# Routing attention and feed-forward block: the first sequence's first layer in written order, a second buffer under the accumulating transfers, and another order at the start

## The chip, the cores and the metric

The kernel runs on one core of one Trainium2 chip. The metric is the device time in microseconds (us); the time before is 976.38 us, the median of 3 runs (975.72 to 977.27). The traced execution spans 973.6 us; all trace times count from its start. TensorE is called PE (PEld for its weight loads), VectorE DVE, ScalarE ACT, GpSimd POOL, SyncE SP. "L387" is line 387 of the kernel before.

## The reference

Attention in which a query sees only the keys whose nearest centroid is the same as its own, then a layer norm and a two-layer feed-forward with a residual:

```python
# q, k, v: (4, 8, 768, 64); centroids: (8, 16, 64)
q_n = q / (norm(q) + 1e-6); k_n = k / (norm(k) + 1e-6); c_n = centroids / (norm(centroids) + 1e-6)
q_assign = argmax(einsum('bhsd,hcd->bhsc', q_n, c_n)); k_assign = argmax(einsum('bhsd,hcd->bhsc', k_n, c_n))
scores = where(q_assign == k_assign, q @ k.T / 8, -1e9)
attn   = softmax(scores) @ v            # -> x: (4, 768, 512)
xn = (x - mean) / sqrt(var + 1e-6) * g_ln
out = x + maximum(xn @ w_ch1, 0) @ w_ch2    # w_ch1: (512, 2048), w_ch2: (2048, 512), float64 in memory
```

## The kernel before

The kernel works through 16 pairs of heads (4 sequences, 4 pairs each) and then, for each sequence, through the feed-forward. Both layers of the feed-forward use a scheme with seven products of half-size blocks instead of eight. The text needs four parts of it.

**The start.** Before the first pair can be masked, the centroids must be normed and turned, similarities computed, the best cluster of every row marked in `onehot`, and that be turned into two mask tiles:

```python
load(0, "q")
nc.scalar.dma_start(out=c_sb, in_=centroids.rearrange("h c d -> (h c) d"))
load(0, "kv")                       # pair 0: halves of q and k alternate on the SP and ACT queues
# ... identity, masks, constants: memsets on GpSimd
def norm_centroids(part):
    if part == 0:   # DVE: squares, sum, lower bound          -> c_ss
    elif part == 1:
        nc.scalar.activation(c_nrm, c_ss, AF.Sqrt)
        nc.scalar.activation(warm, c_nrm, AF.Exp, scale=0.0)   # only brings Exp's table in
    else:           # DVE: five small operations              -> c_sb normed

with tc.manual_schedule(engines=order):      # order = PE, DVE, ACT: these run as written
    norm_centroids(0); prep_transpose(0, 0); load(1, "q")
    norm_centroids(1); prep_transpose(0, 1); load(1, "k")
    norm_centroids(2)
    scores(0, "qk", ("qk",))        # score step 0, its q k product alone
    turn_centroids()
    scores(1, "qk", ("qk",))
    prep_sims(0); prep_turn(0); prep_route(0)       # similarities, turned, one-hot
    prep_transpose(1, 0)            # pair 1's q
    # ... loads
    prep_onehot(0); prep_mask(0, 0); prep_mask(0, 1)    # m on DVE for pair 0; two masks on ACT
    scores(0, "qk", ("mask", "exp")); scores(1, "qk", ("mask", "exp"))
    # ... all 192 score steps, the weighted sums and the weight chunks between them
```

**Weights.** Each of the 32 chunks (128 x 512 float64) is turned into float32 on DVE: the high words give a rounded part that is written to `w`, the low words a rest in `tb`, which a transfer adds to `w`. `tb` is free again when that transfer has landed. 23 chunks are converted in the attention, the last 9 in sequence 0's first layer.

```python
def split_weight(m):                 # three DVE operations
    ta = pools["conv"].tile([P, WC], U32, tag="ta", name="ta")
    tb = pools["conv"].tile([P, WC], U32, tag="tb", name="tb")      # the pool has one buffer
    # L238, L241: ta from the high words;  L244: tb from the high words
def join_weight(m):                  # three more
    # L253: w from ta and tb;  L257: tb from w;  L258: tb from the low words and tb
    nc.gpsimd.dma_start(out=w, in_=fb, accum_op=ALU.add)            # fb is tb read as float32; L261
```

**First layer.** Seven parts for each j of 0 to 7; a product is four matmuls. One bank x takes parts 1, 6, 7 and 4 one after another, and ACT copies it out between them:

```python
def first_layer(b, j, part):
    if part == 1:   product(x, ..., True);  p1 = kept(x)        # kept: ACT copy, L724
    elif part == 2: product(y, ..., True);  add_relu(y + p1)    # DVE add, L729; appended to summed
    elif part == 6: product(x, s2, t2);     u2 = kept(x)
    elif part == 5: product(z, s1, t1, True)
    elif part == 7: product(x, s3, ...);    u3 = kept(x); add_relu(z + u3)
    elif part == 4: product(x, ...);        nc.scalar.activation(hidden, x, AF.Relu)    # L765
    elif part == 3: product(z, s4, ...);    add_relu(z + u2)
def relu(m):        # ACT: ReLU in place over the m oldest of summed, L737
def w1_sums(b, j):  # DVE: four sums of weight blocks s1..s4 for part 6, 5, 7, 3 of j, L572, two buffers
```

**The loop around it.** Only PE's order is fixed here; the scheduler orders DVE, ACT, SP and GpSimd:

```python
with tc.manual_schedule(engines={PE, DVE}):
    # j = 0: parts 1, 2, 6, 5, 7, the sums, the end of the last pair (finish(.., 0))
with tc.manual_schedule(engines={PE}):
    for b in range(B):
        for j in range(NFH):
            if j + 1 < NFH and (b or j): w1_sums(b, j + 1)
            for part, ahead in ((1, 0), (2, 0), (4, 1), (6, 0), (3, 1), (5, 0), (7, 0)):
                if j - ahead >= 0 and (b or j): first_layer(b, j - ahead, part)
            relu(max(0, len(summed) - 3))
            if b == 0 and j in (1, 3): finish(len(pairs) - 1, (j + 1) // 2)
            for m in within.pop(j, ()) if b == 0 else ():    # one chunk each for j = 1, 2, 3, 6, 7; two for 4 and 5
                split_weight(m); join_weight(m); load_weight(m + 2)
        # ... second layer (L802)
```

Of the kernel before, what the change touches and what calls it, by code (L numbers as in the profile page):

```python
# [19 lines left out]
def kernel(  # L20
# [11 lines left out]
    nc = tc.nc  # L32
# [86 lines left out]
    load(0, "q")  # L119

    c_sb = const.tile([H * NCL, D], F32, name="c_sb")
    nc.scalar.dma_start(out=c_sb, in_=centroids.rearrange("h c d -> (h c) d"))
    load(0, "kv")

    ident = const.tile([P, P], F32, name="ident")
# [32 lines left out]
    c_ss = const.tile([H * NCL, 1], F32, name="c_ss")  # L158
    c_nrm = const.tile([H * NCL, 1], F32, name="c_nrm")
    c_tmp = const.tile([H * NCL, 1], F32, name="c_tmp")  # L160
    warm = const.tile([P, 1], F32, name="warm")

    def norm_centroids(part):
        if part == 0:
            nc.vector.tensor_tensor(c_sq, c_sb, c_sb, ALU.mult)
            nc.vector.tensor_reduce(c_ss, c_sq, AX.X, ALU.add)

            nc.vector.tensor_scalar_max(c_ss, c_ss, 2.0 ** -100)
        elif part == 1:
            nc.scalar.activation(c_nrm, c_ss, AF.Sqrt)  # L170

            nc.scalar.activation(warm, c_nrm, AF.Exp, scale=0.0)
        else:

            nc.vector.reciprocal(c_tmp, c_nrm)
            nc.vector.scalar_tensor_tensor(
                out=c_tmp, in0=c_tmp, scalar=c_ss, in1=c_nrm, op0=ALU.mult, op1=ALU.add
            )
            nc.vector.tensor_scalar(c_nrm, c_tmp, 0.5, 1e-6, op0=ALU.mult, op1=ALU.add)
            nc.vector.reciprocal(c_tmp, c_nrm)  # L180
            nc.vector.tensor_scalar_mul(c_sb, c_sb, c_tmp)
# [50 lines left out]
    def split_weight(m):  # L232
        words = raws[m].bitcast(U32).rearrange("p (n w) -> p n w", w=2)
        hi = words[:, :, 1]
        ta = pools["conv"].tile([P, WC], U32, tag="ta", name="ta")
        tb = pools["conv"].tile([P, WC], U32, tag="tb", name="tb")

        nc.vector.tensor_scalar(  # L238
            ta, hi, 0x07FFFFFF, 3, op0=ALU.bitwise_and, op1=ALU.logical_shift_left
        )  # L240
        nc.vector.scalar_tensor_tensor(  # L241
            out=ta, in0=hi, scalar=0xC0000000, in1=ta, op0=ALU.bitwise_and, op1=ALU.bitwise_or
        )
        nc.vector.tensor_single_scalar(tb, hi, 0x7FF00000, op=ALU.bitwise_and)  # L244
        halves[m] = (ta, tb)
# [84 lines left out]
    def prep_onehot(n):  # L330
# [8 lines left out]
                )  # L339

        m = heads.tile([P, S], BF16, tag="m", name="m")
        if n:
            nc.scalar.activation(m, t[:, :S], AF.Identity, bias=far[:, 0:1], scale=far[:, 1:2])
        else:
            nc.vector.tensor_scalar(
                m, t[:, :S], far[:, 1:2], far[:, 0:1], op0=ALU.mult, op1=ALU.add
            )
        z = mask[n % 2]
        prepared[n]["oh"] = t
        prepared[n]["m"] = [(z[:D], m[:D]), (m[D:], z[D:])]  # L350
# [1 line left out]
    def prep_mask(n, j):  # L352
        t, z = prepared[n]["oh"], mask[n % 2]
        src, dst = ((D, 0), (Q, D + Q))[j]
        src, dst = slice(src, src + NCL), slice(dst, dst + NCL)
        nc.scalar.activation(  # L356
            z[dst], t[src, :S], AF.Identity, bias=far[src, 0:1], scale=far[src, 1:2]
        )

# [242 lines left out]
    with tc.manual_schedule(engines=order):  # L604
# [4 lines left out]
        prep_transpose(0, 1)  # L609
        load(1, "k")  # L610
        norm_centroids(2)
        scores(0, "qk", ("qk",))
        turn_centroids()
        scores(1, "qk", ("qk",))
        prep_sims(0)
        prep_turn(0)
        prep_route(0)
        prep_transpose(1, 0)
        load(2, "q")
        load_weight(0)  # L620
        load_weight(1)
        prep_onehot(0)
        prep_mask(0, 0)
        prep_mask(0, 1)
        scores(0, "qk", ("mask", "exp"))
        scores(1, "qk", ("mask", "exp"))
        for u in range(len(pairs) * slots):
            n, slot = divmod(u, slots)
            nxt = n + 1 < len(pairs)
# [222 lines left out]
            add_store(b, 0, tt, 1, st["u2", tt], st["z", tt])  # L852


    with tc.manual_schedule(engines={mybir.EngineType.PE, mybir.EngineType.DVE}):
        first_layer(0, 0, 1)
        first_layer(0, 0, 2)
        first_layer(0, 0, 6)
        finish(len(pairs) - 1, 0)
        w1_sums(0, 0, (2, 3))  # L860
        x_sum(0, 3)
        first_layer(0, 0, 5)
        first_layer(0, 0, 7)
        x_sum(0, 4)
        w1_sums(0, 1)

    with tc.manual_schedule(engines={mybir.EngineType.PE}):
        for b in range(B):
            st = {}
            if b:  # L870
                w1_sums(b, 0)
            for j in range(NFH):
                if j + 1 < NFH and (b or j):
                    w1_sums(b, j + 1)
                for part, ahead in ((1, 0), (2, 0), (4, 1), (6, 0), (3, 1), (5, 0), (7, 0)):
                    if j - ahead >= 0 and (b or j):
                        first_layer(b, j - ahead, part)
                relu(max(0, len(summed) - 3))
                if b == 0 and j in (1, 3):
                    finish(len(pairs) - 1, (j + 1) // 2)  # L880
                for m in within.pop(j, ()) if b == 0 else ():
                    split_weight(m)
                    join_weight(m)
                    load_weight(m + 2)
            if b == 0:
                rest.close()
                ffn = pool("ffn", 2)
            relu(len(summed))
# [240 lines left out]
```

## Time and profile before

| engine | busy, us | share of the span | instructions |
|---|---|---|---|
| PE | 945.2 | 97% | 4614 |
| PEld | 576.8 | 59% | 4614 |
| DVE | 611.1 | 63% | 1102 |
| ACT | 349.8 | 36% | 557 |
| POOL | 77.4 | 8% | 146 |

Busy time is the time in which an engine has an instruction under way; for PE, whose matmuls overlap, a busy stretch may still run at a lower granted clock. The mean granted clock is 0.988. In a line of the timeline stand the start and the length in us, engine, source line, operation, output and inputs, shapes, how many were merged, and in brackets the idle time of the engine before it with what ended it. A line of the waits holds who waited for whom, the time in all, how often, and the longest. The stages of the span: the start (0 to 24 us), the attention (to 366), sequence 0's first layer (to 456), its second layer and the three other sequences (to the end).

### The profile page before, as it was taken

How to read it: one execution, taken by the hardware profiler on the slowest of the kernel's cores; microseconds unless marked ns; L12 is line 12 of the kernel's file. 1: busy time of each engine (PE TensorE's matmuls, PEld its weight loads, DVE VectorE, ACT ScalarE, POOL GpSimd, SP SyncE). 2: the span in 40 equal slices, each digit the busy share in tenths (PEclk: the TensorE clock that was granted, in tenths of full speed). 3: DMA queues.
4: the chain of work that ended last, by engine and by line, in shares of the span. 5: the costliest groups of instructions: out<-in, count | busy, mean ns of one | idle time of the engine just before them, and what ended most of it. 6: DMA issues, size and time to landing. Idle time of an engine off the chain costs nothing.

```text
span 973.6 us, 12451 instructions
## 1 busy us (share of the span) xinstructions
PE 945.2 (97%) x4614; PEld 576.8 (59%) x4614; DVE 611.1 (63%) x1102; ACT 349.8 (36%) x557; POOL 77.4 (8%) x146
## 2 busy tenths in 40 slices
PE   5999999999999999888999999999999999999997
PEld 2444444444344445445888556888556888556886
DVE  3788889988798876665967344563344563344431
ACT  4666667667666662222100333000333000333000
POOL 1011212111112121111000000000000000000000
PEclk8999999999999999999999999999999999999999
DMA  7368789987887433542553000211000211000011
GB/s 174 82 150 208 179 191 206 209 181 161 158 168 150 111 77 93 130 98 54 168 173 103 1 0 2 96 66 65 1 1 5 92 66 66 1 0 6 29 39 39
DMA packets 178324, 92.48 MB, mean 95 GB/s; under 512 B 144352, under 2 KB 160848, under 8 KB 178256
## 3 DMA queue, kind: packets, MB, share of 16 engines
q1 hardware_dynamic: 168800, 76.20, 31.3%
q0 software_dynamic: 7712, 14.99, 7.6%
q8 instruction: 38, 0.62, 0.3%
q10 hardware_dynamic: 1744, 0.43, 0.2%
q14 instruction: 30, 0.25, 0.1%
HBM read 64.10 MB, written 19.10 MB: 85 GB/s over the span
## 4 chain that ended last, share of the span: by engine, by line
PE 88%; DMA 4%; issue 4%; DVE 1%; ACT 1%; POOL 0%; ACTq 0%; SPq 0%; POOLq 0%; DVEq 0%
PE s_ps L387 17%; PE x_ps L802 17%; PE a_ps L399 14%; PE x_ps L709 13%; PE z_ps L802 9%; PE z_ps L709 7%; PE y_ps L802 4%; PE y_ps L709 3%; DMA w<-tb 2%; PE den_ps L436 1%; PE sim_ps L293 1%; PE oh_ps L335 1%; PE simT_ps L309 1%; PE qk_ps L276 1%; DMA q_sb<-in_q_dram 1%
## 5 line engine op out<-in xcount | busy, mean ns | idle before, releaser
L382 ACT ACTIVATE e<-s_ps 128x768 f32<-128x768 f32 x192 | 151.6, 809 | 65.5 <-PE s_ps L387 64.4
L387 PE MATMUL s_ps<-t,t 64*128 64x384 f32 x768 | 158.1, 490 | 0.0
L399 PE MATMUL a_ps<-e,v_sb 128*64 128x384 f32 x768 | 144.8, 499 | 0.0
L416 DVE TENSOR_TENSOR es<-es,e 128x768 f32<-128x768 f32 x128 | 121.7, 951 | 21.1 <-ACT e L382 15.7
L737 ACT ACTIVATE h<-h 128x384 f32<-128x384 f32 x96 | 50.2, 523 | 166.8 <-DVE h L729 166.8
L399 PEld LDWEIGHTS a_ps<-e,v_sb 128*64 128x64 f32 x768 | 46.7, 136 | 88.2 <-issue 72.2
L802 PE MATMUL x_ps<-w2t,h 128*128 128x256 f32 x384 | 84.5, 379 | 0.0
L387 PEld LDWEIGHTS s_ps<-t,t 64*128 64x128 f32 x768 | 69.6, 192 | 20.7 <-issue 19.1
L802 PEld LDWEIGHTS x_ps<-w2t,h 128*128 128x128 f32 x384 | 72.7, 190 | 10.1
L387 PE MATMUL s_ps<-m,mask 64*128 64x384 bf16 x192 | 63.6, 331 | 2.8 <-ACT mask L356 1.9
L387 PE MATMUL s_ps<-mask,m 64*128 64x384 bf16 x192 | 63.4, 331 | 0.5 <-ACT mask L356 0.5
L572 DVE TENSOR_TENSOR ws<-w 128x256 f32<-128x256 f32 x64 | 24.5, 418 | 58.4 <-PE z_ps L709 58.4
L709 PE MATMUL x_ps<-xt,w 128*128 128x384 f32 x128 | 49.4, 510 | 7.9 <-ACT u L724 7.9
L729 DVE TENSOR_TENSOR h<-z_ps,u 128x384 f32<-128x384 f32 x64 | 35.2, 551 | 25.5 <-ACT u L724 15.8
L387 PEld LDWEIGHTS <-mask 64*128 64x128 bf16 x192 | 17.9, 94 | 55.9 <-issue 39.6
L709 PE MATMUL x_ps<-xt,ws 128*128 128x384 f32 x128 | 48.9, 506 | 2.1 <-ACT p L724 2.1
L813 DVE TENSOR_TENSOR o_sb<-x_ps,xb 128x256 f32<-128x256 f32 x48 | 20.0, 418 | 48.6 <-PE x_ps L802 48.6
L709 PE MATMUL z_ps<-xn,ws 128*128 128x384 f32 x128 | 47.1, 491 | 1.4 <-DVE h L729 1.4
L709 PE MATMUL x_ps<-xn,ws 128*128 128x384 f32 x128 | 46.7, 488 | 0.6 <-ACT u L724 0.5
L724 ACT COPY p<-x_ps 128x384 f32<-128x384 f32 x32 | 14.8, 464 | 90.1 <-PE x_ps L709 90.1
L709 PE MATMUL x_ps<-xn,w 128*128 128x384 f32 x128 | 46.6, 487 | 0.6 <-ACT late L425 0.6
L709 PE MATMUL z_ps<-xt,ws 128*128 128x384 f32 x128 | 46.6, 487 | 0.0
(137 smaller groups left out, 1378.7 us busy)
## 6 DMA issues: line engine op xcount, KB each, us to landing
raw<-in_moe_w_ch_dram SPq DMA_DIRECT2D x32, 512.0 KB, 4.9
w<-tb POOLq DMA_DIRECT2D x32, 256.0 KB, 5.2
v_sb<-in_v_dram SPq DMA_DIRECT2D x32, 192.0 KB, 3.9
xn<-xT_d SPq DMA_DIRECT2D x16, 384.0 KB, 5.2
xr<-x_d SPq DMA_DIRECT2D x24, 256.0 KB, 2.8
xb<-x_d SPq DMA_DIRECT2D x48, 128.0 KB, 2.2
out_dram<-o_sb SPq DMA_DIRECT2D x48, 128.0 KB, 1.7
k_sb<-in_k_dram SPq DMA_DIRECT2D x62, 96.0 KB, 4.6
```

The lines of the kernel that those rows point to most:

```text
L276: nc.tensor.transpose(t[:, c * P : (c + 1) * P], src[:, g * TH + c, :, :].rearrange("p h d -> p (h d)"), ident,)
L382: nc.scalar.activation(e, s[:, :, :HC], AF.Exp, scale=SCALE)
L387: nc.tensor.matmul(s[:, j, :HC], of_keys[:, keys], of_queries[:, cols], start=part == first, stop=part != first, skip_group_check=True,)
L399: nc.tensor.matmul(acc[j * D : (j + 1) * D, :HC], loaded[n]["v"][:, j, c, :], e[:, j, :], start=(c == 0), stop=(c == NT - 1),)
L416: nc.vector.tensor_tensor(es, es, soft.pop(i), ALU.add)
L572: nc.vector.tensor_tensor(t[:, i], x, y, op)
L709: nc.tensor.matmul(bank[:, :HC], lhs[:, c, :], rhs[:, c, :], start=first and c == 0, stop=c == NDH - 1, skip_group_check=True,)
L724: nc.scalar.copy(t, bank[:, :HC])
L729: nc.vector.tensor_tensor(h, bank[:, :HC], other, ALU.add)
L737: nc.scalar.activation(h, h, AF.Relu)
L802: nc.tensor.matmul(bank[:, :MH], hidden[lhs + (c,)][:, tt * P : (tt + 1) * P], rhs[:, c, :], start=first and c == 0, stop=c == NFH - 1, sk ...
L813: nc.vector.tensor_tensor(o, bank[:, :MH], x, ALU.add)
```

## The change

It is meant to keep PE from waiting in two places: at the start, where the first pair's masks are prepared, and in sequence 0's first layer, where weight chunks are converted beside the products. It does five things:

- the centroids are loaded over GpSimd's queue instead of ACT's;
- Sqrt's table is brought in by an activation on a constant, ahead of everything else on ACT, and the activation that brings Exp's table in no longer reads `c_nrm`;
- turning the centroids, the similarities and the turning of pair 0 come ahead of the first score products, pair 1's q transposes after the first two masked score steps, and pair 0's two masks go from ACT to DVE;
- `tb` gets two buffers;
- sequence 0's first layer is put, unit by unit, into the region whose order holds on PE, DVE and ACT: each chunk's conversion stands in two halves between named parts, and one ReLU after each of the parts 4, 6 and 3. For the other sequences the same function runs with only PE's order fixed.

The diff, cut to its core:

```diff
-    nc.scalar.dma_start(out=c_sb, in_=centroids.rearrange("h c d -> (h c) d"))
+    nc.gpsimd.dma_start(out=c_sb, in_=centroids.rearrange("h c d -> (h c) d"))
...
     warm = const.tile([P, 1], F32, name="warm")
+    nc.vector.memset(warm, 1.0)
+    nc.scalar.activation(warm, warm, AF.Sqrt)
...
             nc.scalar.activation(c_nrm, c_ss, AF.Sqrt)
-            nc.scalar.activation(warm, c_nrm, AF.Exp, scale=0.0)
+            nc.scalar.activation(warm, warm, AF.Exp, scale=0.0)
...
-        tb = pools["conv"].tile([P, WC], U32, tag="tb", name="tb")
+        tb = pools["conv"].tile([P, WC], U32, tag="tb", name="tb", bufs=2)
...
+    def shade(n, out, src, rows):      # used for m and for both masks
+        add, factor = far[rows, 0:1], far[rows, 1:2]
+        if n:
+            nc.scalar.activation(out, src, AF.Identity, bias=add, scale=factor)
+        else:
+            nc.vector.tensor_scalar(out, src, factor, add, op0=ALU.mult, op1=ALU.add)
...
         norm_centroids(2)
-        scores(0, "qk", ("qk",))
         turn_centroids()
-        scores(1, "qk", ("qk",))
         prep_sims(0)
         prep_turn(0)
+        scores(0, "qk", ("qk",))
         prep_route(0)
-        prep_transpose(1, 0)
-        load(2, "q")
...
         prep_mask(0, 1)
+        scores(1, "qk", ("qk",))
         scores(0, "qk", ("mask", "exp"))
         scores(1, "qk", ("mask", "exp"))
+        prep_transpose(1, 0)
+        load(2, "q")
...
+    def first_units(b, j):
+        chunks = within.pop(j, []) if b == 0 else []
+        for part, ahead in ((1, 0), (2, 0), (4, 1), (6, 0), (3, 1), (5, 0), (7, 0)):
+            if chunks and part in (1, 3):
+                split_weight(chunks[0])
+            if j >= ahead:
+                first_layer(b, j - ahead, part)
+            if part in (4, 6, 3):
+                relu(1)
+            if chunks and part in (2, 3):
+                m = chunks.pop(0)
+                join_weight(m)
+                load_weight(m + 2)
+            if part == 5 and j + 1 < NFH:
+                w1_sums(b, j + 1)
...
-    with tc.manual_schedule(engines={mybir.EngineType.PE, mybir.EngineType.DVE}):
+    with tc.manual_schedule(engines=order):
         # ... j = 0 as before
+        for j in range(1, NFH):
+            first_units(0, j)
+            if j in (1, 3):
+                finish(len(pairs) - 1, (j + 1) // 2)
```

More of the change, by code (lines that the diff above doesn't have):

```diff
@@ L341, in prep_onehot @@
         m = heads.tile([P, S], BF16, tag="m", name="m")
[L342 to L347, printed above, removed]
+        shade(n, m, t[:, :S], slice(0, P))
         z = mask[n % 2]
@@ L355, in prep_mask @@
         src, dst = slice(src, src + NCL), slice(dst, dst + NCL)
-        nc.scalar.activation(
-            z[dst], t[src, :S], AF.Identity, bias=far[src, 0:1], scale=far[src, 1:2]
-        )
+        shade(n, z[dst], t[src, :S], src)
+    def shade(n, out, src, rows):
[4 more added lines that the diff above has]
+            nc.vector.tensor_scalar(out, src, factor, add, op0=ALU.mult, op1=ALU.add)
     xT_d = [spill.tile([NDC, P, S], F32, name=f"xT_d{b}") for b in range(B)]
@@ L871 @@
                 w1_sums(b, 0)
[L872 to L885, printed above, removed]
+                for j in range(NFH):
+                    first_units(b, j)
+            else:
                 rest.close()
```

## The prediction

> **What bounds the kernel now.** I read the busy table first, then the stages, then the waits of the stages in which TensorE is not full, then the timeline there. The busy table gives PE 945.2 us of a span of 973.6 us, so at most 28 us can come from a better order; no matmul is added or taken away. The stages tell where those 28 us lie (columns: stretch, its length, then the busy time of PE, PEld, DVE, ACT, POOL, then the granted clock):
>
> ```profile
> 0.00:24.00 24.00, 13.96 (x58) 7.17 (x60) 7.17 (x20) 10.48 (x15) 4.85 (x34) 0.81 0.75 176
> 24.00:366.00 342.00, 341.61 (x2300) 142.29 (x2298) 293.59 (x431) 228.81 (x310) 62.13 (x98) 1.00 0.73 159
> 366.00:456.50 90.50, 79.29 (x232) 43.03 (x229) 57.47 (x128) 23.73 (x53) 9.59 (x13) 0.94 0.42 98
> 456.50:464.20 7.70, 6.34 (x25) 4.48 (x24) 5.96 (x14) 1.79 (x4) 0.84 (x1) 1.00 0.35 78
> 464.20:960.00 495.80, 495.80 (x1968) 373.01 (x1967) 245.61 (x510) 84.97 (x176) 0.00 (x0) 1.00 0.15 48
> ```
>
> PE idles 10.0 us in the first 24 us and 12.6 us around the first sequence's first layer (11.2 + 1.4); in the attention and from 464 us on it is full. Both holes also run partly at half clock (0.81 and 0.94). The change touches these two stages and no other.
>
> The size of the second hole follows from a comparison inside the trace. The first layer's units j = 1 to 7 take 81.58 us for sequence 0 (PE timeline, 374.96 to 456.54) and, with the same 196 matmuls, 63.21 us for sequence 1 (539.94 to 603.15), where nothing waits. From there to the 32 matmuls of the second layer the two take 7.66 us (456.54 to 464.20) and 6.03 us (603.15 to 609.18). Lost in sequence 0: 18.37 + 1.63 = 20.0 us. The granted clock explains 5.1 us of it (0.83, 0.93 and 0.73 in the stretches 406-416, 426-436, 436-446, so 0.17 + 0.07 + 0.27 of 10 us); the rest is waiting. The waits of 374.9 to 464.2 and the timeline show who causes it:
>
> ```profile
> ACT h L737 <- DVE h L729: 63.2, 22, 7.5
> DVE tb L244 <- DMA w<-tb: 24.3, 8, 4.9
> PE x_ps L709 <- ACT u L724: 8.4, 5, 3.3
> ```
> ```profile
> 405.50 0.43 DVE L244 TENSOR_SCALAR tb<-raw 128x512 uint32<-128x512 uint32 x1 [4.95 <-DMA w<-tb]
> ...
> 408.77 0.55 DVE L729 TENSOR_TENSOR h<-z_ps,u 128x384 f32<-128x384 f32 x1
> ...
> 409.35 0.52 ACT L737 ACTIVATE h<-h 128x384 f32<-128x384 f32 x1 [7.49 <-DVE h L729]
> ...
> 409.78 0.46 ACT L724 COPY u<-x_ps 128x384 f32<-128x384 f32 x1
> ...
> 410.29 2.52 PE L709 MATMUL x_ps<-xt,w 128*128 128x384 f32 x4 [2.88 <-ACT u L724]
> ```
>
> Read it downwards. DVE stands 4.95 us before L244, because the one tb buffer is still being read by the accumulating transfer. The add of h behind it is late, the ReLU queued on ACT waits 7.49 us for it, the copy of the bank queued behind that ReLU is late, and PE cannot go on in the bank: 2.88 us idle. PE is stopped by ACT and ACT by DVE, but the cause is a transfer.
>
> The first 24 us, in lines of the timeline:
>
> ```profile
> 2.37 1.70 ACTq L111 DMA_DIRECT2D k_sb<-in_k_dram  x2
> 5.89 1.28 ACT L170 ACT_TABLE_LOAD   x1
> 8.94 0.15 DVE L179 TENSOR_SCALAR c_nrm<-c_tmp 128x1 f32<-128x1 f32 x1 [0.66 <-ACT warm L172]
> 11.53 0.85 PE L293 MATMUL sim_ps<-t,cT 128*32 128x384 f32 x8
> 15.24 1.51 PE L276 MATMUL qk_ps<-ident,q_sb 128*128 128x128 f32 x6 [1.69 <-DMA q_sb<-in_q_dram]
> 18.30 1.99 ACT L356 ACTIVATE mask<-oh_ps,far 16x768 bf16<-16x768 bf16 x2 [1.03 <-DVE m L345]
> 21.71 0.48 PE L387 MATMUL s_ps<-m,mask 64*128 64x384 bf16 x1 [0.58 <-ACT e L382]
> ```
>
> It is one chain: centroid norms, similarities (11.53), one-hot (ready 14.74), its turning (16.68), masks (ready 20.29), first exps, third score step (21.71). PE is full from there on, so the stage is worth what this last start moves.
>
> [...] after idle gaps of 2.88 and 3.28 us the weight loads at 412 and 437 us take 0.34 us instead of 0.19. [...] here w<-tb lands 5.2 us after its issue (median), whoever waits, so a second buffer can only hide it. [...] three loads of 1.28 us stand in the first 9 us.
>
> **Part 1, first layer in written order.** The instruction order of PE is unchanged here; DVE, ACT and GpSimd change. A unit is 7 products of 1.29 us, 9.03 us of PE. DVE per unit, by spacing in the timeline: one weight chunk 3.2 us (six operations), three adds 1.4, four sums ws 1.5, together 6.1 us. Units 4 and 5 have two chunks, 9.3 us. Extra: multiply and transpose of late 1.9 us at the end of unit 3, four w2 sums of 0.69, so 2.6 us after unit 4, and 1 us of small reductions. In all some 58 us beside 63.2 us of PE, so it fits, but locally it is tight: through units 4 and 5 DVE has 1.9 + 9.3 + 2.6 + 9.3 = 23.1 us of work beside 18.1 us of PE, 5 us too much. The ws sums for the next unit stand five products, 6.5 us, ahead of their use, minus the 1.5 us that they take, so nearly all of the 5 us is absorbed; placing the operations one after another leaves one PE wait of 0.8 to 1.5 us, at part 6 of unit 6. No other: in the new ACT order each copy stands behind ReLUs whose adds lie at least two adds back, 2.6 us for each copy against 0.47 us of copy. With tb double, L244 waits for the transfer of two chunks before, issued at least 5 us earlier. With one tb buffer the same placement would lose about 10 us, so the buffer is not an ornament. As a test I placed the old order in the same way: it gives units 1 to 7 about 77.4 us at full clock, against 81.58 - 5.1 = 76.5 measured. [...] Units 1 to 7: 63.2 + 1.2 = 64.4, **17.2 us less**.
>
> After unit 7: DVE's hidden sums wait for the last chunk's transfer (memory reuse). It is issued near 437 us on the old time axis and lands near 442; the last add that PE needs then ends before PE wants it at 444.4. So the 1.63 us go as well, perhaps not entirely: I count **1.5 us**.
>
> **Part 2, the start.** The centroid load leaves the ACT queue: the second k load on it starts at 3.7 us now, since the ninth transfer reuses the semaphore of the first (the instruction order with its waits shows it); with eight it can start near 2.3. A Sqrt load moves ahead of the first copy and replaces the load of 4.10; one of three loads goes. warm no longer reads c_nrm, so the 0.66 us wait goes. No score step stands ahead of the centroid turning and the similarities any more: centroids ready 9.57 to about 8.3, cT near 9.3, similarities 11.53 to about 9.5. Then sim copy, turning, maximum and comparison as now (3.2 us): one-hot near 12.6, with the first score step beside it (1.6 us), turned 13.5. m on DVE (0.68) and the two masks on DVE (0.62 each by spacing, instead of 0.99 on ACT behind a 1.0 us wait): ready near 15.5 instead of 20.29. Two exps and pair 1's six transposes follow, and the third score step starts at 17 to 18 instead of 21.71: **3.7 to 4.7 us less**; I take 4.0. Against it: the GpSimd issue (0.92 us, as for g_sb) delays the identity from 2.57 to 3.5 us, just ahead of q's landing at 3.77; and the centroids may land later than 5.32 (g_sb took 5.5 us from issue to landing), which would take back about 1 us.
>
> **Sum.** 976.4 - 17.2 - 1.5 - 4.0 = 953.7; a little more is likely to be left over than placed, so **954 us**, 2.3% less.
>
> **Rivals.** (a) DVE becomes the bound of the first layer: 58 us of 63, units 4 and 5 overfull. If its operations spread by 10%, or a raw chunk lands late behind the scattered x_d stores that SP issues ahead of it, PE loses another 3 to 6 us[...]: 957 to 961. (b) In-order engines turn another wait: the new ACT and DVE orders are fixed, so one late operand holds everything behind it; for it speaks that DVE at the start waits for k of pair 1 (used now at 18.11); against it, its adds are not due before. Worth 1 to 2 us. (c) The start is held by transfers: the DMA share is 0.99 from 5 to 10 us. Then the masks come no earlier, and only the first layer pays: 957.7.
>
> **Range and chances.** The first layer gives 15 to 19.5 us, the start 1.5 to 6 [...]: 950.5 to 960. The 2% line is 956.85 us, 2.9 us above the prediction. Faster by over 2%: 0.8; within 2%: 0.19; slower: 0.01.
>
> **What would show it.** Units 1 to 7 of sequence 0 in 63.5 to 66 us; the DVE wait tb for w<-tb gone from 24.3 us to under 2; PE waits for ACT u and p in that stage from 10.5 us to under 1, and if any is left, one for ws; clock 1.00 from 366 to 460. Masks of pair 0 on DVE near 15 us, the third score step near 17.5. It is wrong if DVE's waits there are short and PE still waits (rival a), or if the similarities do not move from 11.5 us (rival c).

## The result, and the profile after

The changed kernel takes **952.6 us** (median of 4 runs, 952.2 to 955.4) against 976.3 us: a ratio of 0.976, 95% interval 0.974 to 0.978. Measured again later, it was 954.4 against 977.8 us (0.975, 0.974 to 0.977).

The stages of the traced execution, in the columns of the same view before (stretch, its length, busy time of PE, PEld, DVE, ACT, POOL, the granted clock, DMA share, GB/s). The second and third boundaries are moved to where the same work stands now:

```profile
0.00:24.00 24.00, 16.87 (x88) 7.65 (x88) 11.98 (x28) 9.44 (x16) 5.47 (x35) 1.00 0.81 175
24.00:364.30 340.30, 337.56 (x2270) 140.98 (x2270) 290.81 (x426) 226.66 (x307) 62.68 (x98) 1.00 0.74 160
364.30:437.80 73.50, 72.13 (x232) 41.43 (x229) 61.02 (x135) 24.97 (x54) 10.81 (x14) 1.00 0.53 124
437.80:443.90 6.10, 6.10 (x26) 4.60 (x25) 5.93 (x13) 1.49 (x3) 0.00 (x0) 1.00 0.57 178
443.90:940.00 496.10, 496.10 (x1970) 373.27 (x1969) 241.70 (x503) 84.99 (x176) 0.00 (x0) 1.00 0.15 47
```

The third row is the point: sequence 0's first layer takes 73.5 us instead of 90.5, PE is idle 1.4 us of it instead of 11.2, and the clock is 1.00 instead of 0.94. DVE is busy 61.0 of 73.5 us, where it was 57.5 of 90.5. The fourth row is full, where 1.4 us were idle. In the first 24 us stand 88 matmuls instead of 58; the clock of 1.00 in that row is not to be believed (last section). The second row has lost something, 2.7 us of idle PE instead of 0.4; more of that below.

The waits of units 1 to 7 and what follows them (373.5 to 443.9 us), who waited for whom, total, times, longest:

```profile
ACT h L739 <- DVE h L731: 3.7, 4, 1.5
...
PE x_ps L711 <- DVE ws L574: 0.8, 1, 0.8
DVE hs L798 <- DMA w<-tb: 0.5, 1, 0.5
```

L731, L739, L711 and L574 are L729, L737, L709 and L572 of before. The ReLUs' wait for adds has fallen from 63.2 to 3.7 us, DVE's wait for the accumulating transfer ahead of L244 (now L246) is gone from the list, and PE's waits for ACT's copies u and p are gone too. The list has one PE wait. Its place, in the PE timeline and then DVE's:

```profile
423.56 1.53 PE L711 MATMUL x_ps<-xt,ws 128*128 128x384 f32 x4 [0.79 <-DVE ws L574]
```
```profile
420.75 0.68 DVE L255 SCALAR_TENSOR_TENSOR w<-tb,ta 128x512 f32<-128x512 uint32 x1
421.47 0.43 DVE L259 TENSOR_SCALAR tb<-w 128x512 uint32<-128x512 uint32 x1
421.93 0.69 DVE L260 SCALAR_TENSOR_TENSOR tb<-raw,tb 128x512 f32<-128x512 uint32 x1
422.54 0.42 DVE L574 TENSOR_TENSOR ws<-w 128x256 f32<-128x256 f32 x1
422.99 0.42 DVE L574 TENSOR_TENSOR ws<-ws,w 128x256 f32<-128x256 f32 x1
```

It is part 6 of unit 6. DVE has no gap in brackets here: it comes out of the two chunks of unit 5 (conversion operations back to back) and writes the ws block too late. This is a wait for an engine that is full, not for a transfer.

The first 24 us, lines of the timeline after:

```profile
2.92 1.28 ACT L164 ACT_TABLE_LOAD   x1 [2.92 <-issue]
4.87 0.22 DVE L168 TENSOR_TENSOR c_sq<-c_sb 128x64 f32<-128x64 f32 x1 [3.98 <-DMA c_sb<-in_centroids_dram]
5.79 1.28 ACT L174 ACT_TABLE_LOAD   x1
8.51 0.40 PE L191 MATMUL ct_ps<-ident,c_sb 128*64 128x128 f32 x1 [1.03 <-DVE c_sb L183]
9.62 1.51 PE L295 MATMUL sim_ps<-t,cT 128*32 128x384 f32 x8 [0.71 <-DVE cT L194]
```
```profile
14.15 0.82 PE L337 MATMUL oh_ps<-identb,onehot 128*128 128x128 bf16 x6
15.02 0.68 DVE L360 TENSOR_SCALAR m<-oh_ps,far 128x768 bf16<-128x768 bf16 x1 [1.18 <-PE oh_ps L337]
15.71 1.38 DVE L360 TENSOR_SCALAR mask<-oh_ps,far 16x768 bf16<-16x768 bf16 x2
18.36 0.33 PE L389 MATMUL s_ps<-m,mask 64*128 64x384 bf16 x1
20.08 1.51 PE L401 MATMUL a_ps<-e,v_sb 128*64 128x384 f32 x8
```

Two table loads are left of three. Similarities, the one-hot's turning, the masks and the third score step have all moved forward, but not by the same amount. Step by step (us from the start):

| | predicted | before | after | gained so far |
|---|---|---|---|---|
| similarities start | 9.5 | 11.53 | 9.62 | 1.91 |
| one-hot ready | 12.6 | 14.74 | 13.83 | 0.91 |
| its turning starts | | 16.68 | 14.15 | 2.53 |
| masks ready | 15.5 | 20.29 | 17.09 | 3.20 |
| third score step | 17 to 18 | 21.71 | 18.36 | 3.35 |
| first weighted sum | | 25.03 | 20.08 | 4.95 |

### The profile page after: what moved, and what is told of

Its sections match the earlier page's. It is cut to its first block, busy times and chain, and to the rows that moved or that the text cites. A ratio compares the mean times of both kernels' runs of the same rounds, so it can differ in the third digit from the quotient of the medians.

```text
span 953.5 us, 12450 instructions
## 1 busy us (share of the span) xinstructions
PE 936.6 (98%) x4614; PEld 574.5 (60%) x4614; DVE 612.7 (64%) x1105; ACT 347.6 (36%) x555; POOL 79.0 (8%) x147
## 4 chain that ended last, share of the span: by engine, by line
PE 90%; DVE 5%; issue 2%; DMA 2%; ACT 1%; POOL 0%; ACTq 0%; DVEq 0%; POOLq 0%
PE x_ps L804 17%; PE x_ps L711 16%; PE s_ps L389 15%; PE a_ps L401 12%; PE z_ps L804 9%; PE z_ps L711 8%; PE y_ps L804 4%; PE y_ps L711 4%; PE den_ps L438 1%; PE sim_ps L295 1%; DVE es L418 1%; PE simT_ps L311 1%; PE oh_ps L337 1%; PE qk_ps L278 1%; DMA rb<-row 1%
## 5 line engine op out<-in xcount | busy, mean ns | idle before, releaser
L731 DVE TENSOR_TENSOR h<-z_ps,u 128x384 f32<-128x384 f32 x64 | 35.6, 556 | 94.8 <-PE z_ps L711 71.5
L739 ACT ACTIVATE h<-h 128x384 f32<-128x384 f32 x96 | 49.6, 522 | 85.1 <-DVE h L731 85.1
L726 ACT COPY u<-x_ps 128x384 f32<-128x384 f32 x64 | 30.6, 478 | 78.6 <-PE x_ps L711 78.6
L815 DVE TENSOR_TENSOR o_sb<-x_ps,xb 128x256 f32<-128x256 f32 x48 | 20.1, 420 | 51.3 <-PE x_ps L804 48.7
L389 PEld LDWEIGHTS <-mask 64*128 64x128 bf16 x192 | 17.9, 93 | 54.5 <-issue 39.2
L711 PE MATMUL x_ps<-xt,ws 128*128 128x384 f32 x128 | 46.6, 487 | 0.8 <-DVE ws L574 0.8
L711 PE MATMUL x_ps<-xn,w 128*128 128x384 f32 x128 | 46.6, 487 | 0.6 <-ACT late L427 0.6
L711 PE MATMUL z_ps<-xt,ws 128*128 128x384 f32 x128 | 46.6, 487 | 0.0
L711 PE MATMUL z_ps<-xn,ws 128*128 128x384 f32 x128 | 46.5, 486 | 0.0
L711 PE MATMUL x_ps<-xn,ws 128*128 128x384 f32 x128 | 46.5, 486 | 0.0
L711 PE MATMUL x_ps<-xt,w 128*128 128x384 f32 x128 | 46.5, 486 | 0.0
```

What stands on the lines that cost most here:

```text
L389: nc.tensor.matmul(s[:, j, :HC], of_keys[:, keys], of_queries[:, cols], start=part == first, stop=part != first, skip_group_check=True,)
L711: nc.tensor.matmul(bank[:, :HC], lhs[:, c, :], rhs[:, c, :], start=first and c == 0, stop=c == NDH - 1, skip_group_check=True,)
L726: nc.scalar.copy(t, bank[:, :HC])
L731: nc.vector.tensor_tensor(h, bank[:, :HC], other, ALU.add)
L739: nc.scalar.activation(h, h, AF.Relu)
L815: nc.vector.tensor_tensor(o, bank[:, :MH], x, ALU.add)
```

## The experiments

The time of a whole run varies by 0.7 to 6.3 us between executions of one kernel in one measurement, so the verdicts rest on stages read from each kernel's one profile. "First sum" is the start of the first weighted sum; "attention" runs from there to the first layer; "units" from unit 1 to the second layer's first matmul; "on" from there to the 32 matmuls. Times in us, ratio with its 95% interval, each against the kernel before on the same chip.

| kernel | median | ratio | first sum | attention | units | on |
|---|---|---|---|---|---|---|
| before | 976.3 | | 25.03 | 342.7 | 81.27 | 7.66 |
| changed | 952.6 | 0.976 (0.974 to 0.978) | 20.08 | 346.0 | 64.24 | 6.03 |
| first layer only | 958.4 | 0.981 (0.979 to 0.983) | 24.89 | 344.5 | 64.24 | 6.03 |
| start only | 970.5 | 0.995 (0.992 to 0.998) | 20.23 | 345.2 | 80.78 | 6.03 |
| written order, one tb | 965.0 | 0.988 (0.984 to 0.991) | 20.15 | 344.9 | 75.99 | 6.03 |
| old order, two tb | 964.8 | 0.987 (0.985 to 0.989) | 24.42 | 344.7 | 71.08 | 6.03 |
| changed, again | 954.4 | 0.975 (0.974 to 0.977) | 21.67 | 344.4 | 64.24 | 6.03 |
| chunks in one piece | 953.6 | 0.976 (0.974 to 0.977) | 20.13 | 343.7 | 63.54 | 6.03 |
| more work on DVE | 956.2 | 0.979 (0.978 to 0.981) | 20.06 | 344.0 | 66.89 | 6.03 |
| centroids on ACT's queue | 954.7 | 0.976 (0.974 to 0.977) | 20.61 | 344.2 | 64.25 | 6.03 |
| pair 1's q early | 955.8 | 0.978 (0.976 to 0.980) | 22.77 | 345.0 | 64.24 | 6.03 |
| score products early | 955.2 | 0.978 (0.976 to 0.980) | 21.68 | 344.2 | 64.23 | 6.03 |
| masks on ACT | 953.9 | 0.976 (0.974 to 0.978) | 21.62 | 343.4 | 64.24 | 6.03 |
| two moves more | 952.4 | 0.974 (0.972 to 0.976) | 18.96 | 343.9 | 63.21 | 6.03 |

### Each half alone

First layer only: the changed kernel with the old start.

```diff
-    nc.gpsimd.dma_start(out=c_sb, ...)
+    nc.scalar.dma_start(out=c_sb, ...)
... # the tables, the start's order and the masks on ACT as before
```

> The kernel after with its start put back as it was before (centroids over ACT's queue, old warm, old order, masks on ACT); first layer in written order and tb double stay. Theory (two separate holes, the first layer's worth 18.6 us): units 1 to 7 of sequence 0 in 63.9 to 64.1 us, 6.03 us from there to the 32 matmuls, the first 25 us of TensorE as before; 957.5 us. Rival (part of the first layer's gain is owed to the earlier start, since transfers then stand better): units 1 to 7 over 66 us and 960 us or more.

Start only: the kernel before with the new start; one tb, and its first layer ordered by the scheduler.

> The kernel before with the changed start alone; first layer and tb as before. Theory: first weighted sum at 20.1 us instead of 25.0, the first layer's units 1 to 7 again about 81.6 us; 971.4 us. Rival (the first layer takes back what the start gives, since its last chunk loads and transfers do not come earlier): 974 us or more, units 1 to 7 over 84 us.

By the medians the first layer alone brings 17.9 us, the start alone 5.9; together 23.8, and the whole change brings 23.7. Each of these is known to 2 or 3 us only, so that they agree to 0.1 us is luck. The stages (first sum, units and "on") give 18.8 and 6.9 us, together 25.7, against 23.6 for the whole change: the first has units of 64.24 us and a late first sum, the second a first sum at 20.23 and units of 80.78. The two parts do not disturb each other; they meet in one place, the 1.6 us of "on", which each of them gains alone.

One detail went against the prediction: "start only" has the old first layer and one tb, and yet takes 6.03 us from the second layer's first matmul to the 32 matmuls, as every kernel here except the one before. DVE still waits 1.7 us for the last transfer in it, as it did before (1.64); there PE stood 1.36 us behind it, here it does not stand at all. DVE's operations there have the same order in both kernels, but in "start only" DVE starts the add that PE needs 3.7 us after the end of unit 7 (457.41 - 453.75) instead of 5.7 (462.20 - 456.54). So the 1.6 us go when DVE is 2 us further on at that point, and the written order is not the only thing that brings it there; what did so in "start only" stays open.

### The buffer and the order, apart

Written order with one tb:

```diff
-        tb = pools["conv"].tile([P, WC], U32, tag="tb", name="tb", bufs=2)
+        tb = pools["conv"].tile([P, WC], U32, tag="tb", name="tb")
```

> The kernel after with one tb buffer. Theory (both are needed: in written order DVE stands before the third operation of a chunk until the transfer of the chunk before has landed): placing the operations with measured lengths gives units 1 to 7 in 73.0 us plus half-clock time of 1.7 to 5 us, with two waits of about 3 and 7 us at part 6 of units 5 and 6 for the ws sums, and 10.3 us instead of 6.0 to the 32 matmuls: 13 to 18 us more than after, 966 to 970 us. Rival (the order is what counts, the buffer an ornament): within 2 us of after.

Old order with two: the kernel before with this line the other way round, nothing else.

> The kernel before with two tb buffers and nothing else. Theory (most of the first layer's loss is the transfer): placing the operations in the order that the scheduler then gives yields units 1 to 7 in 67.6 us and 6.0 after them, so 14 to 15.6 us of the 20 lost come back: 961 to 963 us; TensorE still waits some 4 us for copies behind ReLUs on ACT. Rival (the scheduler's order is the cause, ReLUs ahead of copies): under 8 us less, 969 us or more.

Units: 81.27 us with neither, 75.99 with the order alone, 71.08 with the buffer alone, 64.24 with both. "The buffer alone" is one edit but two effects. Given two buffers, the scheduler orders DVE otherwise than before: three times it puts a chunk's L244 ahead of L257 and L258 of the chunk before, where with one buffer they never mix. Each alone is well short, and they fail in different ways. DVE's waits and then PE's in the units, first the written order with one tb:

```profile
DVE tb L246 <- DMA w<-tb: 13.4, 6, 4.4
```
```profile
PE x_ps L711 <- DVE ws L574: 8.9, 2, 6.1
```

The transfer stops DVE in its fixed order, the sums ws come late, and PE stands 8.9 us in two waits, 8.1 us more than with two buffers. PE waits here for the sums, not for a copy on ACT. The rest of the 11.75 us goes to the half clock, of which the records hold 10.2 us in two stretches, from 415.6 and 429.3 us on. The whole, 965.0 us, is 1 us below the range that was expected. Next the old order with two tb, the waits of 372 to 456:

```profile
ACT h L737 <- DVE h L729: 54.1, 23, 7.4
...
DVE tb L244 <- DMA w<-tb: 4.3, 4, 1.3
PE x_ps L709 <- ACT u L724: 3.8, 2, 3.4
```

The transfer's wait has fallen from 24.3 to 4.3 us, so the buffer does what it is for. But the ReLUs still stand 54.1 us for adds, and PE still stops 3.4 us at once, with 3.4 us of half clock after it. The timeline at that stop:

```profile
423.92 0.43 DVE L238 TENSOR_SCALAR ta<-raw 128x512 uint32<-128x512 uint32 x1 [2.43 <-DMA raw<-in_moe_w_ch_dram]
425.12 0.43 DVE L244 TENSOR_SCALAR tb<-raw 128x512 uint32<-128x512 uint32 x1 [0.77 <-DMA w<-tb]
...
428.99 0.55 DVE L729 TENSOR_TENSOR h<-z_ps,u 128x384 f32<-128x384 f32 x1
...
429.57 0.52 ACT L737 ACTIVATE h<-h 128x384 f32<-128x384 f32 x1 [7.37 <-DVE h L729]
...
430.00 0.46 ACT L724 COPY u<-x_ps 128x384 f32<-128x384 f32 x1
...
430.51 2.92 PE L709 MATMUL x_ps<-xt,w 128*128 128x384 f32 x4 [3.35 <-ACT u L724]
```

It is the prediction's chain with another transfer at its head. The add stands behind the conversion of a chunk for which DVE has waited 2.43 us for the chunk's own load and 0.77 us for the accumulating transfer; the ReLU waits for the add, the copy stands behind the ReLU, and PE behind the copy. So transfers still hold DVE here, and the order lets it reach PE. In the changed kernel no wait of DVE for a load is left in these units. Whether DVE's written order or ACT's does it was not tried apart. The order alone was expected to leave 10.3 us from the second layer's first matmul to the 32 matmuls: it left 6.03, a miss of my placing. The expectation for the old order with two tb, 961 to 963 us, was also missed, by 2 us (964.8): its units took 71.08 us where the placing had made 67.6, to which the half-clock stretch of 3.4 us adds at most 1.7.

### Halves or one piece

```diff
-            if chunks and part in (1, 3): split_weight(chunks[0])
...
-            if chunks and part in (2, 3): m = chunks.pop(0); join_weight(m); load_weight(m + 2)
...
+        for m in chunks:              # after part 7
+            split_weight(m); join_weight(m); load_weight(m + 2)
```

> The changed kernel, but each weight chunk of sequence 0's first layer is converted in one piece at the end of its unit instead of in two halves between named parts. Theory: what counts is that the order is written and that tb is double; the place of the six operations within the unit matters little, since each product's sums stand 6.5 us ahead of their use. Placing gives units 1 to 7 in 63.4 us with one PE wait of 0.2 us: the same as the changed kernel or up to 0.8 us less. Rival: the halves are what keeps the adds of h in time; then a 3.2 us block of DVE (6.4 in units 4 and 5) holds up adds, ReLUs and copies, and each such unit loses 1 us or more: 5 us or more longer.

Units 63.54 us: the halves buy nothing. The profile's list of PE's waits for this stage is empty, because the ws of the next unit now come ahead of the chunk on DVE instead of behind it, so the 0.79 us wait is gone. ACT's ReLUs wait 8.7 us for adds in these units, the longest time 4.6 us, and PE does not wait at all. That suggests that a late add costs nothing as long as no copy that PE needs at once is queued behind its ReLU; it was not tried by itself. Cutting chunks up is not needed for that.

### How near DVE is to being the bound

```diff
             if part == 5 and j + 1 < NFH:
                 w1_sums(b, j + 1)
+            if part == 5 and b == 0:
+                for i in range(4):       # read by nobody
+                    nc.vector.tensor_tensor(spare[:, i], w1_block(1, 0, j), w1_block(1, 1, j), ALU.add)
```

> The changed kernel with four extra sums of weight blocks on DVE at the end of each of units 1 to 7 of sequence 0's first layer, written to a tile that nobody reads: 4 x 0.35 us a unit by the spacing of such sums, 10 us in all. It asks how close DVE is to being the bound of that stage, as rival (a) of the prediction had it. DVE is busy 55.8 us of the stage's 64.2 in the profile of the changed kernel, and 9.6 of 9.9 in unit 6. Theory: with 10 us more it has 66, more than PE's 63.2, and the excess of units 4 to 6 can no longer slide: units 1 to 7 in 67 to 70 us, with several PE waits for ws or for ACT's copies in units 5 to 7, the whole 3 to 6 us longer. Rival: most of DVE's busy time can slide under PE's lead, and units 1 to 7 stay under 65.5.

```profile
PE x_ps L712 <- DVE ws L575: 2.3, 1, 2.3
PE z_ps L712 <- DVE h L732: 0.9, 1, 0.9
```

The units take 66.89 us, 2.65 more; DVE is busy 63.3 us of them instead of 55.8. That rejects the rival (under 65.5) and misses the expected 67 by a little. Both waits stand in unit 6, at 423.1 and 425.5 us, behind the two units with two chunks; elsewhere the additional work slides under PE. So DVE's limit in this stage is local: about a third of the added busy time (2.65 of 7.5 us) comes out as time, all in one place.

### What carries the start

Four parts of the start were put back one at a time.

Centroids on ACT's queue again:

```diff
-    nc.gpsimd.dma_start(out=c_sb, ...)
+    nc.scalar.dma_start(out=c_sb, ...)
```

> The changed kernel with the centroid load back on ACT's queue; all else as changed. By the theory of the start, the second k load on ACT is then the ninth transfer and starts at about 3.7 us instead of 2.9, and the centroids land near 5.3 instead of 4.9: the similarities 0.4 to 0.8 us later, the whole 0.5 us longer. Rival 1: the identity comes earlier, because GpSimd is not held for 0.9 us by the issue, so the first transposes of q start earlier and the whole is the same or shorter. Rival 2: the k transfer sets the start, and 1.3 us are lost.

Similarities at 10.14 instead of 9.62, first sum at 20.61 instead of 20.08: 0.5 us by the stages, as expected; the whole does not tell it apart from no change. The centroids' own load (32 KB) hardly moved: over GpSimd it was issued at 1.30 us and used at 4.87, over ACT's queue here issued at 1.84 and used at 5.06, only 0.2 us later. What the centroids delay on ACT's queue is k: its second load there is issued at 3.64 us instead of 2.38. In the changed kernel and then here:

```profile
5.87 1.62 PE L278 MATMUL qk_ps<-ident,k_sb 128*128 128x128 f32 x6 [0.32 <-DMA k_sb<-in_k_dram]
```
```profile
6.43 1.53 PE L278 MATMUL qk_ps<-ident,k_sb 128*128 128x128 f32 x6 [0.99 <-DMA k_sb<-in_k_dram]
```

On DVE the last step of the centroids' norms stands behind the copy of these transposes, and starts at 7.81 instead of 7.28 us. So the 0.5 us are k's landing, passed on by DVE's order.

Pair 1's q transposes back ahead of the one-hot's turning:

```diff
         prep_route(0)
+        prep_transpose(1, 0)
+        load(2, "q")
...
         scores(1, "qk", ("mask", "exp"))
-        prep_transpose(1, 0)
-        load(2, "q")
```

> The changed kernel with pair 1's six q transposes (and the load after them) where they stood before the change, after pair 0's turning and ahead of its one-hot, instead of after the first two masked score steps. Theory: PE does them in order, 0.9 us at full clock and 1.6 to 1.7 us at half, ahead of the one-hot's turning; the one-hot is ready at 13.8 in any case, and the products that now stand beside it fill that time, so the turning and the masks come about 1 us later, but the transposes are then gone from the later place: the first weighted sum 0.5 to 1.5 us later, plus 0.7 if the transposes must wait for q of pair 1. Rival: the place of the transposes doesn't matter, since PE is idle 2 to 3 us ahead of the one-hot: the first weighted sum within 0.2 us of 20.1.

```profile
12.53 1.65 PE L389 MATMUL s_ps<-t,t 64*128 64x384 f32 x4
15.51 1.51 PE L278 MATMUL qk_ps<-ident,q_sb 128*128 128x128 f32 x6 [1.33 <-DMA q_sb<-in_q_dram]
16.82 0.85 PE L337 MATMUL oh_ps<-identb,onehot 128*128 128x128 bf16 x6
```

At the turning this is the largest piece. PE stands 1.33 us for pair 1's q, which nobody needs yet, then takes 1.3 us for its transposes, and only then the turning that all the masks wait for, 2.67 us later than in the changed kernel. The first sum is also 2.7 us later, at 22.77; I had expected at most 2.2 us. But PE runs at half speed until 19.8 us here, and in that profile of the changed kernel only until 15.8. Against the second profile of the changed kernel below (half speed until 20.6, first sum at 21.67) it is 1.1 us. So the place of these transposes is worth 1.1 to 2.7 us at the first sum.

The first two score products back ahead of the centroids' turning:

```diff
         norm_centroids(2)
+        scores(0, "qk", ("qk",))
         turn_centroids()
+        scores(1, "qk", ("qk",))
         prep_sims(0)
...
-        scores(0, "qk", ("qk",))     # behind prep_turn(0)
-        scores(1, "qk", ("qk",))     # behind prep_mask(0, 1)
```

> The changed kernel with the first two score products of q and k ahead of the turning of the centroids and of the similarities again, as before the change. Theory: they take 0.8 us each at full clock and 1.6 at half and PE takes them in order, but PE now waits 1.1 us for the normed centroids at that place, which hides part: similarities 0.5 to 2.1 us later (10.1 to 11.7), the first weighted sum later by up to as much, 1.6 us at most. Rival: the time comes back, because the one-hot's 3 us on DVE and ACT then has no score products left to hide beside it: the same, 20.1.

The times look like the rival's. The similarities are 1.16 us later (10.78), but the one-hot's turning starts at 14.05, even 0.1 us earlier, and the masks begin at 15.60 instead of 15.71. The reason is mostly another one, though. From the similarities to the ready one-hot it took 3.21 us here and 4.21 in the changed kernel, because in this execution PE was at full speed by then (similarities 0.85 us instead of 1.51, their turning 0.55 instead of 0.90). The rival's saving is the rest: the turning stands 0.3 us behind a score product in the changed kernel, and 0.06 behind the one-hot here. At half speed, by these lengths, I estimate that the turning would have come about 0.9 us later. So what the place of the score products is worth is not shown: nothing in this execution, up to 0.9 us at equal speed. The first sum, at 21.68, is 1.6 us later; the half-speed stretch shown further below accounts for that.

Pair 0's two masks on ACT (`m` stays on DVE, other than the expectation's first sentence has it):

```diff
-        shade(n, z[dst], t[src, :S], src)
+        nc.scalar.activation(z[dst], t[src, :S], AF.Identity, bias=far[src, 0:1], scale=far[src, 1:2])
```

> The changed kernel with pair 0's m and masks on ACT as for the other pairs' tiles, instead of on DVE. Theory: two masks take 2 x 0.9 to 1.0 us on ACT against 1.4 us in all on DVE, and m one more; the masks' exps stand on ACT behind them: masks ready 0.6 to 1.6 us later, the first weighted sum by as much. Rival: ACT is idle there and takes m beside DVE's copies, so nothing is lost: within 0.2 us.

```profile
13.36 0.82 PE L337 MATMUL oh_ps<-identb,onehot 128*128 128x128 bf16 x6
...
15.00 1.99 ACT L353 ACTIVATE mask<-oh_ps,far 16x768 bf16<-16x768 bf16 x2 [4.11 <-DVE m L362]
```

From the turning's start to ready masks: 16.99 - 13.36 = 3.63 us, against 17.09 - 14.15 = 2.94 on DVE. The place on DVE is worth 0.7 us, at the lower edge of what was expected. The first sum cannot tell it: by the clock records PE changed its speed five times in this execution ahead of it (the four matmuls of a score product took 1.65 us at 11.78, 0.98 at 14.11 and 1.49 at 19.05).

### The changed kernel again, and two moves more

> The changed kernel once more, beside the next three on the same chip. Its profile is to tell whether the attention, which took 345.96 us from the first weighted sum to the first layer in the first profile of the changed kernel and 342.72 us in that of the kernel before, is longer by the change. If it is the change, 345 to 346 again; if it varies from execution to execution, anything from 342.7 to 346, and the whole within 951 to 954. Start (first weighted sum at 20.1 us) and units 1 to 7 (64.24 us) as before, to 0.1 us.

The attention took 344.4 us in this profile and 346.0 in the first. Its code is the same in all kernels here, and it took 343.4 to 346.0 us in all but the kernel before, whose one profile has 342.7, with the old start (344.5, 344.7) as with the new, with one tb as with two. In the first profile of the changed kernel 1.7 us of it are one PE wait for a one-hot at 163.6 us, behind a wait of DVE for a transfer (1.87 us, rb<-row), in a part where the DMA share is 0.9 and more. So it varies between executions and is no effect of the change that these runs could show; whether the old kernel's is shorter on average, one profile cannot tell.

That the start would be the same to 0.1 us was a miss: the first sum in this profile is 1.6 us later than in the first one, although the one-hot's turning is at the same place (14.19 and 14.15). Score products in it:

```profile
14.95 1.65 PE L389 MATMUL s_ps<-t,t 64*128 64x384 f32 x4
...
19.67 1.26 PE L389 MATMUL s_ps<-t,t 64*128 64x384 f32 x4
20.93 0.81 PE L389 MATMUL s_ps<-t,t 64*128 64x384 f32 x4
```

The same product takes 1.65 us up to 16.6 us and 0.81 at 20.9. The clock records have PE at half speed until 20.6 us, and 1.26 us for the product that starts at 19.67 fits that. In the first profile the full 0.81 is there at 18.5 already. "Score products early" (half clock recorded from 13.92 for 6.83 us) and "masks on ACT" (from 17.69 for 3.41 us) have the same delay.

The last kernel is the changed one with two operations moved, one against the wait of unit 6, one against PE's wait of 1.03 us for the normed centroids:

```diff
         norm_centroids(1)
+        norm_centroids(2)            # was behind the two lines that follow
         prep_transpose(0, 1)
         load(1, "k")
...
         for j in range(1, NFH):
             first_units(0, j)
+            if j == 6:
+                w2_sum(first_st, 1)  # was behind unit 7
```

> The changed kernel with two operations moved. (1) The second sum of w2 blocks, which stood after unit 7 of the first sequence's first layer, stays with its four operations but goes to the end of unit 6, so the second layer's start needs less of DVE; (2) the last step of the centroid norms stands on DVE ahead of the copy of pair 0's second transposes. My theory, that DVE's written order alone sets both places: the wait of 0.8 us for ws at part 6 of unit 6 goes only if the order ahead of it becomes lighter, so I expect units 1 to 7 in 63.2 to 64.2 us, and the first weighted sum about 1 us earlier (19.1): 1 to 2 us less than the changed kernel in all. Rival: the start hangs on the transfers of q and k, and the centroids are not what ends the wait there: the first weighted sum stays at 20 us, and the whole within 0.5 us of the changed kernel.

Its PE timeline around the centroids:

```profile
7.42 0.39 PE L191 MATMUL ct_ps<-ident,c_sb 128*64 128x128 f32 x1
8.52 1.51 PE L295 MATMUL sim_ps<-t,cT 128*32 128x384 f32 x8 [0.71 <-DVE cT L194]
```

Turning (8.51 in the changed kernel) and similarities (9.62) are 1.1 us earlier, the first line has no wait in brackets, and the first sum is at 18.96 instead of 20.08: this piece of the start hung on DVE's order and not on a transfer. Units 1 to 7 take 63.21 us, exactly what sequence 1's take, and the list of PE's waits for this stage is empty. By the stages it is 2.1 us less than the changed kernel (1.12 and 1.03), and the medians of the two, measured together, differ by as much, 952.4 and 954.4 us, but their intervals overlap (0.972 to 0.976 and 0.974 to 0.977). It beats the kernel before; that it beats the changed kernel is shown in its stages, not in its whole time.

## Why the prediction was right, and where it was not

**What bounds.** The two places were right: the change moved these two stages, and their gains add up but for the 1.6 us behind unit 7. "At most 28 us can come from a better order" was not a limit, since it counts idle PE alone: with the same 4614 matmuls PE's busy time fell from 945.2 to 936.6 us, above all because less of it runs at half clock (in the first layer's stage, with 232 matmuls before and after, 79.3 us at a granted clock of 0.94 became 72.1 at 1.00). In the first profiles the gains of the stages are 17.0, 1.6 and 4.95 us, 23.6 in all, and the longer attention takes 3.3 of them back; the spans differ by 20.1 us, the medians by 23.7.

**First layer, 17.2 us less to 64.4.** Measured: 64.24, with one PE wait of 0.79 us for ws, at part 6 of unit 6 as placed, and a granted clock of 1.00. That both halves of the change are needed is shown by the two kernels in which one was left out. Of the chain that the prediction read downwards (transfer, DVE, ReLU on ACT, copy, PE), the old order with two tb still shows all links from DVE on; in the written order with one tb the transfer reaches PE by another way, the sums ws. "The cause is a transfer" said too little: with that wait cut from 24.3 to 4.3 us, PE still stopped 3.4 us at once. "Not an ornament" holds: it said about 10 us for one tb, and 11.75 were measured. The sum of DVE's work was added up wrongly: the items listed make 54.6 us, not 58, and 55.8 were measured. The starting value was 0.3 us too high: 374.96 was the weight load's start, unit 1's first matmul starts at 375.28, so the units before took 81.27 us and the gain is 17.0.

**After unit 7, 1.5 us.** 7.66 became 6.03 us, 1.63. The size was right. The reason was too narrow, since "start only", with the old first layer, shows 6.03 us as well.

**The start, 4.0 us.** 4.95 measured in the first profile, 3.4 in the second. The sum was near for two errors that point in opposite ways. The term that was mis-sized is "sim copy, turning, maximum and comparison as now (3.2 us)": they took 13.83 - 9.62 = 4.21 us. The similarities now run at half speed: 1.51 us for them instead of 0.85, and 0.90 instead of 0.55 for their turning, which is the 1.0 us. The new order is not by itself the reason, as one might think. In the first two kernels below the start is written as before the change; in the last it is the new one but for the masks:

```profile
11.62 1.51 PE L293 MATMUL sim_ps<-t,cT 128*32 128x384 f32 x8
```
```profile
11.70 1.51 PE L293 MATMUL sim_ps<-t,cT 128*32 128x384 f32 x8
```
```profile
9.47 0.85 PE L295 MATMUL sim_ps<-t,cT 128*32 128x384 f32 x8 [0.71 <-DVE cT L194]
```

These are "old order, two tb", "first layer only" and "masks on ACT"; to the ready one-hot it takes 4.22, 3.87 and 3.57 us in them. So the 3.2 us were the length of this piece in one execution that had come to full speed early, and "as now" took them for fixed. With 0.3 us for the score product that the turning stands behind, the masks were ready 1.6 us later than predicted, and the third score step came at 18.36, later than the 17 to 18. The other error is that I read the gain at the third score step and took everything behind it as fixed. From there to the first weighted sum it was 3.32 us before, at half speed, and 1.72 in the first profile after. PE was at half speed until 25.0 us before, until 15.8 in this profile. The sum had no term for the clock. That the start came out 1 us above the 4.0 in the first profile and 0.6 below in the second is this speed, and luck.

**Among the parts of the start** the prediction gave no shares. By the runs, the place of pair 1's q transposes is worth 1.1 to 2.7 us, the masks on DVE 0.7, the centroids' queue 0.5; for the score products it is not shown. The tables were not tried alone.

**The rivals.** (a) DVE as the bound: not reached, at 55.8 us busy of 64.2 (58 was estimated), but 7.5 us of busy time more costs 2.65 us, so it is near, in units 4 to 6. (b) Another wait by the fixed order: one, 0.8 us. (c) The start held by transfers: not as forecast, since the similarities moved 1.9 us. In part it is: PE waits 0.3 us for k, and k's later landing alone costs the 0.5 us of "centroids on ACT's queue".

## What to carry to other kernels

Where an engine waits for a transfer to give a buffer back, look at two things at once: that buffer, and the order of what is queued behind the waiting instruction on this engine and the next. Here each alone gave 5 to 10 us, both 17. On an engine that takes its work in order, an early place for work whose operand arrives late (pair 1's q, 1.33 us of waiting) costs all that stands behind it. And a length read from one execution carries the clock of that execution with it (the similarities took 0.85 us in one, 1.51 in another): before it goes into a sum "as now", compare the same operation elsewhere in the trace, or take a second profile.

## What the runs showed that was not expected

PE's half speed in the first 25 us is not one stretch with a fixed end. By the clock records, the first profile of the changed kernel comes to full speed at 15.8 us, the second of the same kernel at 20.6. Over all kernels with the new start it was 13.8 to 16.3 us in seven profiles, 19.8 and 20.6 in two, and 7.5 in "masks on ACT"; with the score products ahead of the similarities 10.5, 11.4, 13.1 and, in "old order, two tb", 24.3. That these products bring full speed early is not shown: three of the four profiles were early, and one was the latest of all. And early full speed did not last. The kernel before had it from 11.4 to 14.8 us, then half speed until 25.0; "score products early" had it from 10.5 to 13.9, then half speed until 20.8. In "masks on ACT" (full speed from 7.5 us) four matmuls of a score product took 1.65 us again at 11.78, in "first layer only" (from 13.1 us) 1.51 at 21.85. A late end cost up to 1.6 us, more than the masks' and the centroids' moves together.

What makes PE fall to half speed, these runs do not settle. In the kernel before, one fall came at 410.73 us, 0.44 us after PE's gap of 2.88 us had ended, and one at 434.62, 0.64 us ahead of the end of the gap of 3.28 us; half speed then lasted 3.41 and 6.83 us. The fall at 14.78, with 10.24 us of half speed behind it, had only a gap of 0.62 us ahead of it and 1.23 us of the gap of 1.69 us that ends at 15.24: in its 3.41 us at full speed PE was busy 1.56. In "two moves more" PE was busy 2.4 of the first 3.4 us after its rise and stayed at full speed. Nor do these runs settle why two executions of one kernel rise 4.8 us apart.

The clock column shows 1.00 for the first 24 us after the change, although PE was at half speed until 15.8 us (four matmuls of a score product took 1.65 us at 12.57, 0.81 at 18.54): the records begin with the first change, and the column takes the time ahead of it as full. So at the start the durations of one and the same product are the better reading.
